# Attention steps in twos, the projection ahead of the weighted sums, and routing in short operations

## The chip, the cores and the metric

The kernel runs on one core of a Trainium2 chip. Its time is that of one execution on the device, in microseconds (us). PE is the matrix engine (TensorE), DVE the vector engine, ACT the scalar engine, POOL the GpSimd engine, and SP the engine that issues most of the DMAs. Each engine works through its own queue in the order in which the program was written.

## What is computed

Attention over 4 batches of 8 heads, 768 tokens, head size 64, in which a query sees only the keys whose six sign bits (of a projection on six columns) agree with its own; then a mixture of experts on the result:

```python
q_bits = (einsum('bhsd,dk->bhsk', q, proj) > 0)
k_bits = (einsum('bhsd,dk->bhsk', k, proj) > 0)
mask = q_bucket[:, :, :, None] == k_bucket[:, :, None, :]
scores = where(mask, q @ k.T / sqrt(64), -1e9)
attn = softmax(scores)
x = (attn @ v) as (3072, 512)
e_idx = argmax(x @ w_gate)
for each expert e:
    out[rows of e] = gate * sigmoid(x @ w_output_gate)[e] * (relu(x @ w1[e]) @ w2[e])
```

All in 32-bit floats; the scores are matched to that with two-part operands (a high and a low half).

## The kernel before

**The attention stage** works on 16 pairs of heads. A pair has 12 steps of 128 queries by 768 keys, so there are 192 steps (`NSTEP`), in 32 blocks of six (`PER`). For one step s:

- `scores(s)` (L538) is the score tile, called S below: eight matmuls (four products, each as two that run side by side in the two 64-row halves of the array) fill the two banks of a `ps_s` tile. DVE's minimum (L550) brings it to SBUF as `sc` and gives each row's smallest value. There are two `ps_s` tiles, used in turn.
- `soft` (L553) is ACT's exponential in place, with the row sums; `normal` (L562) is for two steps: DVE adds up the sums and takes the reciprocal (L565, L566), and POOL scales both tiles (L568).
- `transposed(s - 6, ...)` (L570), called T below, turns the scaled tile of six steps earlier: twelve matmuls with the identity (L589), six to a 64-row half, each half into a bank of its own. The first half always goes to one of two `ps_t` banks, the second to `ps_m` or `ps_a` (or `ps_t`). Two ACT copies (L595), of the second half first, bring them to `pts`.
- `weighted` (L598), called W below, makes the weighted sums of the block before, once per block: six column blocks for each of the two heads j=0 and j=1, side by side, in a `ps_a` bank; DVE copies the result to `ot` (L609).

The order of all this is written out by hand in one loop over the steps (L972 to L1002): S of the step, then, at the first step of a block (k == 0), five exponentials, the scalings and W, then T of six steps earlier, then whatever was planned for this step. Two lists carry everything else: `plan(step, fn)` runs a function after the step's T; `block(step, when, fn)` runs it at a block's first step, at the place named by `when`. Before the change these places are "early" and "amid" (ahead of and between the scalings), then "logits", "matmuls" (W, and behind it the projection) and "behind" (DMAs).

What else the steps carry, and what the change touches:

- `project` (L432): the sign bits of a later pair of heads, four matmuls into `ps_m`, a threshold on DVE (L443), then the bits' DMAs in `spread` (L525).
- `routing(b)` (L628): for each batch but the last its experts' logits (L640), their transposes in `tokens` (L650), the best expert (`best`, `choose`), the prefix sums over tokens (`prefix`, L707 to L712), ranks, positions (`table_chunks`, `table_pos`) and the table that lists each expert's tokens (`table_rhs`, `table_hot`, `table_sum` L238, `table_add` L241). They are planned at fixed steps counted from the batch's end, s0.
- From step 168 on (`late`), the first expert is chosen (`compare`, `pick`, `chosen`), its first weights are loaded and split in eight pieces on POOL (`early_w1`, L917 and L918), and its first tokens are gathered and turned (`early_gather`, `early_turn`).
- `rows` (L611) puts finished sums into `xb` (DVE, two buffers) and from there into `x_dram` by SP's DMAs.

The experts proper, which follow the attention stage, are not touched.

## Time and profile before

| | us |
|---|---|
| median of 3 runs (lowest to highest) | 725.77 (725.47 to 726.86) |
| the profiled execution, its own time | 729.64 |
| its span, first to last instruction | 727.8 |
| PE busy | 713.2 (98%) |
| DVE, ACT, POOL busy | 462.6, 456.1, 398.5 |

The span is one execution as the hardware profiler saw it, 1.8 us shorter than that execution's own time. A row of the timeline gives an instruction's start, its duration, its engine and line, what it writes and reads, and in brackets how long the engine stood idle before it and what ended that. Matmuls overlap, and the ends of PE's instructions are modelled, so the distance between two starts says more than a duration.

### The profile page before, as it was taken

Reading aid. Unit: us, or ns where it says so; the run is one execution under the profiler, and the core shown is the slowest. Engines: PE = TensorE matmul, PEld = TensorE weight load, DVE = VectorE, ACT = ScalarE, POOL = GpSimd, SP = SyncE. Lnnn points to the kernel's source line nnn. Section 1 sums busy time; section 2 is a strip of 40 time slices with the busy share of each in tenths; the row PEclk is TensorE's granted clock in tenths of the full one; section 3 lists DMA queues with packets and bytes.
Section 4 is the critical chain, followed back from the end, with each engine's and each line's share of the span. In section 5 each row is a group of like instructions: output and inputs, shape, how many; then the busy total and the mean of one; then the engine's idle time right before and its main releaser. Section 6 shows DMA issues by size and latency. Waiting matters only on the chain. (4 is left out here: it accounts for less than half of the span.)

```text
span 727.8 us, 17398 instructions
## 1 busy us (share of the span) xinstructions
PE 713.2 (98%) x6591; PEld 584.1 (80%) x6591; DVE 462.6 (64%) x1008; ACT 456.1 (63%) x927; POOL 398.5 (55%) x489
## 2 busy tenths in 40 slices
PE   8999999999999999999999999999999999999996
PEld 5777785777777777767686689789999999989894
DVE  7877776887767886868976672373554546455440
ACT  5898988898889897988888212442434343434331
POOL 5767756566565666564689525517173636465201
PEclk9999999999999999999999899999999999999998
DMA  5554553444354444542534322744445353537401
GB/s 171 149 129 104 123 129 91 110 104 107 102 126 88 99 121 94 120 102 68 128 61 113 117 68 79 269 137 155 145 135 172 114 189 129 187 118 236 160 11 42
DMA packets 85284, 89.20 MB, mean 123 GB/s; under 512 B 57167, under 2 KB 67591, under 8 KB 85192
## 3 DMA queue, kind: packets, MB, share of 16 engines
q1 hardware_dynamic: 79704, 74.59, 38.3%
q0 software_dynamic: 5200, 13.31, 5.5%
q8 instruction: 54, 0.88, 0.5%
q14 instruction: 38, 0.31, 0.2%
q10 hardware_dynamic: 288, 0.10, 0.1%
HBM read 59.57 MB, written 13.11 MB: 100 GB/s over the span
## 5 line engine op out<-in xcount | busy, mean ns | idle before, releaser
L568 POOL TENSOR_SCALAR sc<-sc,rsum 128x768 f32<-128x768 f32 x192 | 173.2, 916 | 137.3 <-PE ps_a L589 76.8
L550 DVE TENSOR_SCALAR_CACHE_REDUCE sc<-ps_s 128x768 f32<-128x768 f32 x192 | 183.4, 956 | 48.4 <-PE ps_s L547 43.7
L558 ACT ACTIVATE sc<-sc,mn 128x768 f32<-128x768 f32 x192 | 178.4, 937 | 5.3 <-DVE sc L550 5.3
L547 PE MATMUL ps_s<-kh,qhl 64*128 64x384 f32 x768 | 152.2, 379 | 0.6 <-DVE sc L550 0.6
L606 PE MATMUL ps_a<-pts,vt 128*64 128x384 f32 x768 | 137.4, 490 | 0.0
L589 PEld LDWEIGHTS ps_t<-ident,sc 64*128 64x128 f32 x1236 | 95.9, 140 | 26.8 <-POOL sc L568 16.4
L606 PEld LDWEIGHTS ps_a<-pts,vt 128*64 128x64 f32 x768 | 68.6, 137 | 57.6 <-issue 13.9
L595 ACT COPY pts<-ps_t 128x384 f32<-128x384 f32 x203 | 98.0, 490 | 14.8 <-PE ps_t L589 14.8
L589 PE MATMUL ps_t<-ident,sc 64*128 64x64 f32 x1236 | 104.6, 226 | 2.3 <-POOL sc L568 1.6
L335 DVE SCALAR_TENSOR_TENSOR hl<-ps_s,hh 128x256 fp32r<-128x256 f32 (+8 forms) x40 | 34.0, 849 | 107.9 <-ACT hh L334 82.5
L324 PE MATMUL ps_s<-xh,w1h 128*128 128x256 f32 (+7 forms) x288 | 97.3, 338 | 0.0
L345 POOL DMA_INDIRECT out_dram<-yo,sid x29 | 31.1, 1074 | 119.8 <-ACT yo L342 81.1
L324 PE MATMUL ps_s<-xlo,w1h 128*128 128x256 f32 (+7 forms) x288 | 95.7, 332 | 0.0
L324 PE MATMUL ps_s<-xh,w1l 128*128 128x256 f32 (+7 forms) x288 | 95.4, 331 | 0.0
L298 POOL DMA_INDIRECT xq<-x_dram,idx x75 | 81.7, 1089 | 23.8 <-issue 21.3
L334 ACT ACTIVATE hh<-ps_s 128x256 fp32r<-128x256 f32 (+8 forms) x40 | 29.1, 726 | 99.0 <-PE ps_s L324 71.8
L547 PEld LDWEIGHTS ps_s<-kh,qhl 64*128 64x128 f32 x768 | 81.1, 190 | 4.8 <-DVE sc L550 1.7
L547 PE MATMUL ps_s<-bb 64*128 64x384 f32 x384 | 69.3, 338 | 0.0
L547 PE MATMUL ps_s<-kl,qhl 64*128 64x384 f32 x384 | 68.4, 335 | 0.0
L595 ACT COPY pts<-ps_a 128x384 f32<-128x384 f32 x109 | 52.3, 480 | 24.9 <-PE ps_a L589 21.4
L589 PE MATMUL ps_a<-ident,sc 64*128 64x64 f32 x654 | 59.3, 224 | 1.9 <-DVE ot L609 1.9
L589 PEld LDWEIGHTS ps_a<-ident,sc 64*128 64x128 f32 x654 | 54.2, 138 | 4.4 <-DVE ot L609 2.9
(224 smaller groups left out, 1368.5 us busy)
## 6 DMA issues: line engine op xcount, KB each, us to landing
w_raw<-in_w_dram SPq DMA_DIRECT2D x34, 512.0 KB
qk<-in_qkT_dram SPq DMA_DIRECT2D x32, 384.0 KB
qhl<-qhl SPq DMA_DIRECT2D x62, 192.0 KB
xh<-in_w_dram SPq DMA_DIRECT2D x14, 512.0 KB
xlo<-in_w_dram SPq DMA_DIRECT2D x14, 512.0 KB
vt<-in_v_dram SPq DMA_DIRECT2D x16, 384.0 KB
x_dram<-xb SPq DMA_DIRECT2D x60, 96.0 KB
bb<-bt SPq DMA_DIRECT2D x62, 36.0 KB
```

What stands on the lines that cost most here:

```text
L298: nc.gpsimd.indirect_dma_start(out=xq[:, k * P:(k + 1) * P], out_offset=None, in_=x_dram.rearrange("n (a f) -> (n a) f", a=NB32), in_offse ...
L324: nc.tensor.matmul(ps, l, r, start=first and k == 0, stop=last and k == len(pairs) - 1)
L334: nc.scalar.activation(hh, ph, AF.Relu)
L335: return lambda: nc.vector.scalar_tensor_tensor(hl, ph, 0.0, f32(hh), ALU.max, ALU.subtract)
L345: nc.gpsimd.indirect_dma_start(out=out[:, :], out_offset=bass.IndirectOffsetOnAxis(ap=sid[0:n, r, a:a + 1], axis=0), in_=yo[0:n], in_offse ...
L547: nc.tensor.matmul(ss[:, h, 0:HS], q[rs, c:c + P], k[rs, 0:HS], start=(i == 0), stop=(i == 3))
L550: nc.vector.tensor_scalar(sc, ss[:, :, 0:HS], MASKED, None, ALU.min, ALU.min, accum_out=mn)
L558: nc.scalar.activation(pr, pr, AF.Exp, bias=mn, scale=-1.0, accum_out=sums[s // GROUP][:, k, 0:1])
L568: nc.gpsimd.tensor_scalar(live[s0 + k], live[s0 + k], rs[:, k:k + 1], 0.0, ALU.mult, ALU.add)
L589: nc.tensor.transpose(trs[h][:, c], pr[r, c * P:(c + 1) * P], ident[r, r])
L595: (nc.vector.tensor_copy if h and last else nc.scalar.copy)(pts[:, :, t * P + h * hq:t * P + (h + 1) * hq], trs[h])
L606: nc.tensor.matmul(st["av"][j * D:(j + 1) * D], st["v"][:, j, c], blocks[hb][j][:, c], start=(c == 0), stop=(c == NT - 1))
```

## The change

- The loop runs over pairs of steps from step 6 on: S, S, then (at a block's first pair) the exponentials, the projection, the routing's matmuls and W, then T, T, then both steps' plans. All six exponentials of a block come at its first pair.
- The second half of the first T of a block goes to a `ps_s` tile, and DVE, not ACT, copies it; the others take `ps_m` in steps 1, 2 and 4 of a block and `ps_a` in 3 and 5. `sc` gets an eighth buffer; `xb` loses one of two, and the positions' table `t_ob` shares the logits' tile `lt`.
- The projection is at place "before" (ahead of W, behind S), in a `ps_t` bank. So are the logits, the tokens' transposes, the prefix sums and the table's sum, tokens and table in `ps_t` banks.
- The routing's DVE and POOL work is cut into shorter functions, planned by a list of steps (`ROUTE`).
- The choice of the first expert, its loads and its eight pieces on POOL get other steps.

```diff
+        ROUTE = ((18, "best"), (18, "equal"), (20, "lowest"), (20, "one_hot"), (24, "own_ranks"), (26, "chunk_hot"),
+                 (28, "chunk_pos"), (30, "gate_sums"), (32, "hot0"), (33, "column2"), (34, "gate_values"),
+                 (38, "hot1"), (38, "column0"), (39, "column1"), (40, "hot2"))
...
-            sc = tp.tile([P, 2, HS], F32, name="sc", bufs=LAG + 1)
+            sc = tp.tile([P, 2, HS], F32, name="sc", bufs=LAG + 2)
...
-                second = (ps_t, "ps_t") if last or s in held and s % PER == 0 else (
-                    ps_m, "ps_m") if s % 2 == 0 and s not in held else (ps_a, "ps_a")
-                trs = [pool.tile([P, HS], F32, name=name) for pool, name in ((ps_t, "ps_t"), second)]
+                trs = [ps_t.tile([P, HS], F32, name="ps_t")]
+                if s % PER == 0 and not last:
+                    trs.append(ps_s.tile([P, 2, 512], F32, name="ps_s")[:, 0, 0:HS])
+                else:
+                    pool, name = (ps_t, "ps_t") if last else (ps_m, "ps_m") if s % PER in (1, 2, 4) else (ps_a, "ps_a")
+                    trs.append(pool.tile([P, HS], F32, name=name))
...
-                (nc.vector.tensor_copy if h and last else nc.scalar.copy)(
+                (nc.vector.tensor_copy if h and (last or s % PER == 0) else nc.scalar.copy)(
...
-                st["xb"] = gp.tile([P, S // 32, 32], F32, name="xb", bufs=2)
+                st["xb"] = gp.tile([P, S // 32, 32], F32, name="xb", bufs=1)
...
+            def hot_part(h):
+                st["ob"] = table_hot(gp, st["pos"], NT, st.get("ob"), h * NT // 3, (h + 1) * NT // 3)
...
-                    block(s0 - PER, "matmuls", lambda g=g: project(g))
-                    held.add(s0 - PER - LAG)
+                    block(s0 - PER, "before", lambda g=g: project(g, ps_t.tile([P, HS], F32, name="ps_t")))
...
-                block(s0 + PER * (hf + 1), "logits", lambda r=r, hf=hf: r["logits"](hf, H // 2))
-            block(s0 + 3 * PER, "amid", r["choose"])
-            if b < B - 2:
-                block(s0 + 4 * PER, "amid", r["gate_sums"])
-                block(s0 + 5 * PER, "amid", r["gate_values"], r["chunk_pos"])
-            else:
-                block(s0 + 5 * PER, "amid", r["gate_sums"], r["gate_values"], r["chunk_pos"])
-            plan(s0 + 34, r["columns"])
-            block(s0 + 6 * PER, "amid", r["hot"])
-            for n, fn in ((s0 + 8, lambda r=r: r["tokens"](0, H // 2)), (s0 + 14, lambda r=r: r["tokens"](1, H // 2)),
-                          (s0 + 15, r["best"]), (s0 + 20, r["prefix"]), (s0 + 21, r["offsets"]),
-                          (s0 + 22, r["own_ranks"]), (s0 + 23, r["chunk_hot"]),
-                          (s0 + 38, r["table"]), (s0 + 39, r["entries"])):
-                plan(n, fn)
+                block(s0 + PER * (hf + 1), "before", lambda r=r, hf=hf: r["logits"](hf, H // 2))
+            for n, when, name in ((12, "before", "tokens0"), (18, "before", "tokens1"), (24, "before", "prefix"),
+                                  (24, "before", "offsets"),
+                                  (42, "before", "table"), (42, "before", "entries")):
+                block(s0 + n, when, r[name])
+            for n, name in ROUTE:
+                plan(s0 + n, r[name])
...
-        block(late, "amid", compare, pick, chosen)
-        plan(late + 16, early_gather)
+        plan(late + 1, compare)
+        plan(late + 2, pick, chosen)
+        plan(late + 18, early_gather)
...
-            plan(late + (0, 1, 15, 18)[cc], lambda cc=cc: early_load(cc))
+            plan(late + (2, 3, 11, 15)[cc], lambda cc=cc: early_load(cc))
             for h in range(2):
-                plan(late + 12 + (1, 2, 3, 5)[(2 * cc + h) % 4] + PER * (cc // 2), lambda cc=cc, h=h: early_w1(cc, h))
+                plan(late + (8, 10, 13, 14, 16, 19, 20, 22)[2 * cc + h], lambda cc=cc, h=h: early_w1(cc, h))
...
+            for s in range(PER, NSTEP + LAG, 2):
+                k = s % PER
+                both = range(s, s + 2)
+                for x in both:
+                    if x < NSTEP:
+                        live[x] = scores(x)
+                        raw.append(x)
+                if k == 0 and s > PER:
                     softs(2)
                     now("early")
                     normals()
                     now("amid")
                     softs(2)
                     normals()
-                    for when in ("logits", "matmuls", "behind"):
+                    for when in ("before", "matmuls", "behind"):
                         now(when)
-                    softs(0 if s in few else 1)
-                elif k == 4:
+                    softs(1)
+                elif k == 4 or s == PER:
                     normals()
-                if s >= LAG:
-                    transposed(s - LAG, live.pop(s - LAG))
-                if k == 2 and s > 2 * PER or s - 1 in few or PER < s < 2 * PER and k in (1, 2, 4):
+                for x in both:
+                    transposed(x - LAG, live.pop(x - LAG))
+                if s < 2 * PER or k == 0:
                     softs(1)
-                for fn in at.get(s, ()):
-                    fn()
+                for x in both:
+                    for fn in at.get(x, ()):
+                        fn()
```

## Rows read from the trace of the kernel before

**Rows 1.** Windows: stretch, its length, then busy us of PE, PEld, DVE, ACT, POOL, clock, DMA.
```profile
20.00:395.00 375.00, 371.58 (x4666) 277.66 (x4662) 289.05 (x753) 326.12 (x751) 241.18 (x324) 1.00 0.46 108
395.00:410.20 15.20, 13.63 (x124) 10.39 (x123) 7.39 (x16) 9.30 (x18) 14.90 (x15) 0.78 0.59 165
```
**Rows 2.** PE timeline of a steady step: start us, duration us, engine, line, operation.
```profile
251.72 0.21 PE L589 MATMUL ps_t<-ident,sc 64*128 64x64 f32 x1
...
251.78 0.22 PE L589 MATMUL ps_t<-ident,sc 64*128 64x64 f32 x1
...
252.06 0.42 PE L547 MATMUL ps_s<-kh,qhl 64*128 64x384 f32 x2
...
252.85 0.21 PE L589 MATMUL ps_t<-ident,sc 64*128 64x64 f32 x1
```
**Rows 3.** PE timeline: the weighted sums of a block behind logits, and without them.
```profile
221.94 4.09 PE L606 MATMUL ps_a<-pts,vt 128*64 128x384 f32 x24
...
246.25 4.36 PE L606 MATMUL ps_a<-pts,vt 128*64 128x384 f32 x24
```
**Rows 4.** PE timeline at start-up: the last of two score tiles in a row.
```profile
17.52 0.34 PE L547 MATMUL ps_s<-kh,qhl 64*128 64x384 f32 x2
...
18.22 0.53 PE L589 MATMUL ps_t<-ident,sc 64*128 64x64 f32 x12
```
**Rows 5.** ACT timeline ahead of the sums at 246.25.
```profile
245.61 0.48 ACT L595 COPY pts<-ps_a 128x384 f32<-128x384 f32 x1 [0.30 <-PE ps_a L589]
245.99 0.48 ACT L595 COPY pts<-ps_t 128x384 f32<-128x384 f32 x1
```
**Rows 6.** Waits from 100 to 395: who, for whom: us in total, times, longest.
```profile
DVE sc L550 <- PE ps_s L547: 35.2, 77, 1.9
...
PEld ps_a L606 <- ACT pts L595: 8.4, 23, 0.6
...
PE ps_a L589 <- DVE ot L609: 1.9, 4, 1.1
```
**Rows 7.** PE timeline: a transposition followed by the tokens' transposes.
```profile
228.27 0.28 PE L589 MATMUL ps_t<-ident,sc 64*128 64x64 f32 x2
...
228.76 0.55 PE L650 MATMUL ps_m<-ident,lt 128*128 128x128 f32 x3
```
**Rows 8.** DVE timeline: score minima.
```profile
18.30 0.95 DVE L550 TENSOR_SCALAR_CACHE_REDUCE sc<-ps_s 128x768 f32<-128x768 f32 x1
...
253.05 0.96 DVE L550 TENSOR_SCALAR_CACHE_REDUCE sc<-ps_s 128x768 f32<-128x768 f32 x1
...
366.49 0.96 DVE L550 TENSOR_SCALAR_CACHE_REDUCE sc<-ps_s 128x768 f32<-128x768 f32 x1 [0.60 <-PE ps_a L589]
367.37 0.08 DVE L550 DVE_READ_ACCUMULATOR sc<-ps_s 128x1 f32 x1
367.37 0.95 DVE L550 TENSOR_SCALAR_CACHE_REDUCE sc<-ps_s 128x768 f32<-128x768 f32 x1
```
**Rows 9.** DVE timeline: the routing's longer operations.
```profile
138.15 0.56 DVE L680 TENSOR_TENSOR oneh<-ei,expi 128x48 f32<-128x48 f32 x1
138.75 0.84 DVE L683 CAST ohb<-oneh 128x48 bf16<-128x48 f32 x1
...
345.33 0.81 DVE L202 TENSOR_TENSOR t_ge<-rank,chki 128x30 f32<-128x30 f32 x1
346.18 0.44 DVE L205 TENSOR_TENSOR t_oa<-t_ge 128x24 f32<-128x24 f32 x1
```
**Rows 10.** PE timeline behind the last scores.
```profile
402.74 0.90 PE L589 MATMUL ps_t<-ident,sc 64*128 64x64 f32 x12 [1.57 <-POOL sc L568]
```
**Rows 11.** POOL timeline behind the last scores.
```profile
399.81 0.63 POOL L917 TENSOR_SCALAR w1h<-w_raw 128x512 fp32r<-128x512 f32 x1
...
401.77 3.55 POOL L568 TENSOR_SCALAR sc<-sc,rsum 128x768 f32<-128x768 f32 x4
```
**Rows 12.** PE timeline at start-up: a score tile that waited for its bank.
```profile
19.30 0.44 PE L547 MATMUL ps_s<-kh,qhl 64*128 64x384 f32 x2 [0.56 <-DVE sc L550]
```

More of the change, by code (lines that the diff above doesn't have):

```diff
@@ L646, in tokens @@
                     st["lgt"] = gp.tile([P, NT, 2 * E], F32, name="lgt")
-                pm = ps_m.tile([P, 3, H // 2, 32], F32, name="ps_m")
+                pm = ps_t.tile([P, 3, H // 2, 32], F32, name="ps_t")
                 for t in range(3):
@@ L672, in best, with equal, lowest, one_hot @@
                 nc.scalar.activation(st["en"], lgt[:, :, E:2 * E], AF.Exp, scale=-1.0)
-            def choose():
-                eq = gp.tile(bc, F32, name="eq")
+            def equal():
+                st["eq"] = eq = gp.tile(bc, F32, name="eq")
                 nc.vector.tensor_scalar(eq, st["df"], 0.0, None, ALU.is_equal)
                 nc.vector.tensor_tensor(eq, eq, expi[:, None, :].broadcast_to(bc), ALU.mult)
-                ei = gp.tile([P, NT], F32, name="ei")
-                nc.vector.tensor_reduce(ei, eq, AX.X, ALU.min)
-                nc.vector.tensor_tensor(oh, ei[:, :, None].broadcast_to(bc),
+            def lowest():
+                st["ei"] = ei = gp.tile([P, NT], F32, name="ei")
+                nc.vector.tensor_reduce(ei, st["eq"], AX.X, ALU.min)
+            def one_hot():
+                nc.vector.tensor_tensor(oh, st["ei"][:, :, None].broadcast_to(bc),
                                         expi[:, None, :].broadcast_to(bc), ALU.is_equal)
@@ L683, in choose @@
                 nc.vector.tensor_copy(st["ohb"], oh)
+            def choose():
+                equal()
+                lowest()
+                one_hot()
             def gate_sums():
@@ L739, in places, with columns, column @@
                 chunk_pos()
-            def columns():
-                st["rhs"] = table_rhs(gp, st["oa"], oh, gate[:, ts], toki[:, ts], NT, nc.vector if b == B - 1 else nc.gpsimd)
+            def columns(which=(2, 0, 1)):
+                st["rhs"] = table_rhs(gp, st["oa"], oh, gate[:, ts], toki[:, ts], NT,
+                                      nc.vector if b == B - 1 else nc.gpsimd, st.get("rhs"), which)
+            def column(i):
+                columns((i,))
             def cols():
@@ L756, in entries @@
                 table_add(tacc_e, st["pt"])
-            fns = dict(logits=logits, tokens=tokens, add_pair=add_pair, best=best, choose=choose,
+            fns = dict(equal=equal, column0=lambda: column(0), column1=lambda: column(1), column2=lambda: column(2),
+                       tokens0=lambda: tokens(0, H // 2), tokens1=lambda: tokens(1, H // 2), lowest=lowest, one_hot=one_hot, hot0=lambda: hot_part(0), hot1=lambda: hot_part(1),
+                       hot2=lambda: hot_part(2), logits=logits, tokens=tokens, add_pair=add_pair, best=best, choose=choose,
                        gates=gates, prefix=prefix, ranks=ranks, cols=cols, hot=hot, table=table, entries=entries,
@@ L787, in lsh_attention_then_moe @@
                 plan(4, lambda: project(1))
-                held.add(0)
                 plan(5, lambda: split_lo(1, 0, 0), lambda: spread(1, 0))
@@ L824, in lsh_attention_then_moe @@
         for hf in range(2):
-            block(s0 + PER * (hf + 1), "logits", lambda hf=hf: r["logits"](hf, lp))
-            plan(s0 + PER * (hf + 1) + 2, lambda hf=hf: r["tokens"](hf, lp))
-            held.add(s0 + PER * (hf + 1) + 2 - LAG)
+            block(s0 + PER * (hf + 1), "before", lambda hf=hf: r["logits"](hf, lp))
+        block(s0 + 2 * PER, "before", lambda: r["tokens"](0, lp))
+        plan(s0 + 2 * PER + 5, lambda: r["tokens"](1, lp))
         late = 12 * (H // 2) * (B - 1) + 24
@@ L951, in lsh_attention_then_moe @@
             raw = []
-            few = []
             def softs(n):
@@ L970, in now @@
                     fn()
-            for s in range(NSTEP + LAG):
-                k = s % PER
-                if s < NSTEP:
-                    live[s] = scores(s)
-                    raw.append(s)
+            for s in range(PER):
+                live[s] = scores(s)
+                raw.append(s)
                 if 0 < s < 3:
                     turn_idle(3)
-                if s < PER:
-                    normals()
-                    softs(1)
-                elif s < 2 * PER:
-                    if k in (0, 4):
-                        normals()
-                elif k == 0:
+                normals()
+                softs(1)
+                for fn in at.get(s, ()):
+                    fn()
[7 more added lines that the diff above has]
+                if k == 0 and s > PER:
                     softs(2)
```

27 lines of the change are left out of this document (15 added, 12 removed).

## The prediction

> **What bounds the kernel now.** I read the windows first, then the PE timeline of one steady step, then what PE waits for, then the queues that feed it. Between 20 and 395 us the attention stage keeps PE at work for 371.6 of 375.0 us at the full clock [rows 1]; DVE (289 us) and ACT (326 us) have room. So PE's own order is the bound, and 3.4 us at most are plain idle. A PE that counts as busy may still be badly ordered, so I went into the step. A scaled tile's transposition (T, twelve matmuls) takes 0.34 us from its first start (251.72) to the first score matmul; the score tile (S, eight matmuls) takes 0.79 us from there (252.06) to the next T (252.85): 1.13 us a step [rows 2]. The other part of a six-step block is the weighted sums (W, 24 records), 4.36 us; where the logits' matmuls stand in front of W it lasts 4.09 us [rows 3].
>
> **The change, part by part.** The sum is made in the profiled execution's time, 729.64 us, which is 0.5% above the median of 725.77.
>
> *Twos.* Where S follows S with no T between (start-up), it takes 18.22 - 17.52 = 0.70 us, not 0.79 [rows 4]: going over from T to S costs 0.09. Two transposition pairs within T start 0.06 apart [rows 2], so a T followed by T takes 6 x 0.06 = 0.36, not 0.34. Two steps therefore go from 2 x 1.13 = 2.26 to 0.36 + 0.34 + 0.79 + 0.70 = 2.19 us. There are three such pairs in a block and 31 blocks with both kinds of work: 93 x 0.07 = **6.5 us gained**. Bounds: 0.09 each if the second T also takes 0.34 (8.4 gained), and 0.02 each lost if S behind S stays at 0.79 in the steady stretch (1.9 lost). I take 6.5, since both pitches have rows.
>
> *W starts clean.* W's first half (j=0) and second half (j=1) run side by side; j=1 needs the last ACT copy of the block's last T. That copy starts at 245.99 and lasts 0.48, so it ends at 246.47, 0.22 us after W's first matmul at 246.25 [rows 3, 5]: the halves start staggered, and W ends late by that. The trace has 23 such waits of PE on ACT's copies [rows 6], and the W behind logits, whose copies are long done, is 0.27 us shorter. After the change two S stand between the last T and W. Copies run at a pitch of 0.38 [rows 5], and a T's first copy starts 0.26 us after the T: at 245.61, where the S in front of W had begun some 0.9 us before 246.25. The first T of a pair ends 0.36 before the first S, so four copies start 0.10 before that S and end 3 x 0.38 + 0.48 later, at 1.52; the two S last 0.79 + 0.70 = 1.49 us, and the step over to W comes on top. The stagger goes: 23 x 0.27 = **6.2 us gained**; bounds 0 (the copies come later) and 6.2.
>
> *Small matmuls ahead of W.* T followed by the routing's transposes takes 0.49 us (228.27 to 228.76) [rows 7] against 0.34 in front of S [rows 2]. Fourteen such places (seven of tokens, three of prefix, three of the table sum, one of logits) move to between S and W, where the step from S to other work is paid already: 14 x 0.15 = **2.1 us gained**; bounds 0 and 2.1. The projection's matmuls, threshold on DVE and bits stay as many; only their place moves by one W. Its bits and the DMAs behind them ("behind", on SP) come no later than before.
>
> *Routing in short operations.* In the new order a pair lasts 2.19 us and holds two score minima on DVE at a pitch of 0.88 (366.49 to 367.37) [rows 8], so 2.19 - 1.76 = 0.43 us are free per pair; anything longer planned in a pair whose scores come next delays PE. The steps with number 18 and 24 of a batch fall behind W, where DVE has time; those of 28, 34 and 40 fall ahead of W, which covers them. Exposed are one_hot at 20 (0.56 + 0.84, at POOL's side, less 0.43: 1.0) and chunk_hot at 26 (0.81 + 0.44 - 0.43 = 0.8), three times each [rows 9]: 5.4 us. The choice of the expert is exposed once before and once after, and cancels. What these replace is the idle time of now, 3.4 us [rows 1]: **2.0 us lost**. Bounds: 3.4 gained (nothing exposed) and 5.4 lost (nothing of today's idle time goes).
>
> *POOL at the end of attention.* After the last scores PE waits 1.57 us for POOL's scaled tiles (402.74) [rows 10]; POOL had a piece of the first expert's weights (its first operation at 399.81) in front of the last four scalings, which start 1.96 us later at 401.77 [rows 11]. The mean granted clock from 395 to 410.2 is 0.78 [rows 1]: some 6.7 of these 15.2 us went at 1.2 GHz instead of 2.4, which can have cost at most half of that, 3.3 us. The change puts two of the eight pieces a block earlier and leaves three, not four, in the last one; its loads move with them on SP's queue (steps 2, 3, 11, 15 of that stretch), behind the choice's register load, with nothing else urgent behind. I count the piece's 1.96 us and a third of the slow clock, 1.0 us: **3.0 us gained**; bounds 0 and 5.3.
>
> *At nothing.* One of twelve ACT copies per block goes to DVE. DVE does it behind W's own copy, while two T run; if DVE is late there, see the third rival. ACT's six exponentials now stand together around W; ACT works for 326.1 of 375 us today [rows 1] and gives 31 copies of 0.48 away, so 311 us of work meet a stretch of some 362 us, and it still fits. The one buffer of xb waits for DMAs issued a block (11 us) earlier; the shared tile "lt" is written again 14 steps after its last reader.
>
> Sum: -6.5 - 6.2 - 2.1 + 2.0 - 3.0 = -15.8, so 713.8 us profiled; scaled to the median, 725.77 x 713.8 / 729.64 = **710.0 us**.
>
> **Where a page would say otherwise.** The pair is tight on DVE. S's first tile is done 0.79 us after its start, DVE begins 0.20 later (252.85 to 253.05), and the bank is free 1.00 after DVE's start (18.30 to 19.30) [rows 2, 8, 12]. The second minimum thus starts at 0.99 + 0.88 = 1.87 and frees its bank at 2.87; the next pair wants it at 2.19 + 0.79 = 2.98. Slack: 0.11 us. The Trainium skill, page "VectorE: DVE Perf Modes", section "The DRAIN you can't avoid", says that the next DVE operation does not start until the pipe of the one before is empty. By that, the pitch would be no less than the operation's 0.95 us with its accumulator read of 0.08, the bank would be free at 0.99 + 1.03 + 1.00 = 3.02, and two pairs of each block would stall by 0.04: 62 x 0.04 = 2.5 us lost. The trace disagrees: 0.88 is less than the operation's own 0.95 to 0.96, so the sum goes by 0.88.
>
> **The rivals.** *DVE paces the pairs.* If a minimum costs 1.03 and each pair also carries a small operation's 0.3 us (the reciprocal of the sums, a routing step), DVE needs 2 x 1.03 + 0.3 = 2.36 against 2.19: 0.17 lost in the two pairs per block that no W covers, 62 x 0.17 = 10.5, so 724.3 profiled, 720.5. For it: the slack is 0.11 and bursts leave no second reserve. Against: in the steady stretch DVE sat waiting for PE's scores 77 times, 35.2 us [rows 6]. Chance 0.15.
>
> *It doesn't do what it says.* S behind S stays at 0.79 and W keeps its stagger, because the copies of two T crowd against it: without 6.5 and 6.2 the change is -3.1, so 726.5 profiled, 722.7. Against: both have rows. Chance 0.06.
>
> *The borrowed score bank, slower than before.* The block's first T now writes half into a score bank, DVE must empty it, and the block's fourth S needs that bank. DVE's copy stands behind the sums' copy, and both behind whatever DVE waits for (POOL's split, ACT's exponentials). Counted from W's end, S wants the bank at 0.70 + 0.79 = 1.49 us (two T, one S), and a DVE on time frees it at about 0.20 + 2 x 0.48 = 1.16 us (an estimate: DVE's start behind PE from [rows 8], its copies taken like ACT's of the same size [rows 5]). What DVE is late beyond 0.33 stops PE in each of 31 blocks; 0.33 + 15.8/31 = 0.84 is the point from which the kernel gets slower. The trace has PE waiting for the sums' copy up to 1.1 us, four times in all [rows 6]. If that became the rule: 31 x (1.1 - 0.33) = 23.9 lost, 737.7 profiled, 733.8. Against: four times in some 25 blocks, not each. Chance 0.08.
>
> **How the numbers follow.** The forecast, 710.0 us, has 0.71. The unknown terms move it by -3 to +8 us by themselves. The range, 704 to 724 us, takes these in, with the first rival and the second; the third is left out. A difference under 0.2% (1.5 us) is about what a measurement of this kernel can't tell from none. Faster 0.86 (forecast, first rival, most of the second), same 0.05, slower 0.09.
>
> **What would show it.** Right: S behind S at 0.70 and pairs of 2.19 us in the PE timeline; W at 4.1 us in nearly all blocks; no PE waits on ACT's copies ahead of W; attention's last scores some 12 us earlier than now; a higher clock in the last block. DVE's sums' copy starting with W's end in each block speaks against the third rival. Wrong: PE waiting for DVE at the second S of a pair (first rival), W still at 4.36 (second), or PE waiting at the fourth S of each block for a DVE copy of transposed scores (third).

## The result and the profile after

The changed kernel takes **718.44 us** (median of four runs, 716.74 to 719.31) against 726.32 us of the kernel before on the same chip: a ratio of 0.989 [0.9866, 0.9914]. The time lies inside the range and has the sign that was forecast, but the gain of 7.9 us is half of the 15.8 us of the sum. The profiled execution took 719.2 us, with a span of 717.5.

The windows of the changed kernel (stretch, its length, busy us of PE, PEld, DVE, ACT, POOL, clock, DMA) answer to [rows 1], with two more at the start:
```profile
20.00:395.00 375.00, 369.10 (x4725) 261.25 (x4725) 302.20 (x797) 314.74 (x729) 248.37 (x332) 1.00 0.47 111
395.00:410.20 15.20, 14.41 (x137) 10.82 (x136) 11.63 (x23) 5.11 (x12) 6.95 (x7) 1.00 0.40 119
16.00:20.00 4.00, 2.74 (x29) 2.13 (x25) 3.75 (x9) 2.67 (x6) 2.35 (x3) 1.00 0.61 208
20.00:24.00 4.00, 3.60 (x39) 3.55 (x41) 2.81 (x9) 2.27 (x5) 2.34 (x4) 0.62 0.56 117
```
PE is still the bound. ACT fell from 326 to 315 us (311 by the sum) and DVE rose from 289 to 302. The slow clock behind 395 us is gone (1.00 for 0.78; the same work comes some 6 us earlier now, and from 385 to 425 us the clock is 1.00 throughout), but a new stretch at 0.62 has come up between 20 and 24 us.

The PE timeline of the changed kernel (start us, duration us, engine, line, operation, idle time before it and what ended it):
```profile
15.25 0.85 PE L444 MATMUL ps_m<-qk,pjc 128*32 128x384 f32 x8
...
18.63 0.44 PE L552 MATMUL ps_s<-kh,qhl 64*128 64x384 f32 x2 [0.91 <-DVE sc L555]
20.40 0.27 PE L597 MATMUL ps_s<-ident,sc 64*128 64x64 f32 x1 [0.75 <-DVE sc L555]
...
30.10 1.19 PE L614 MATMUL ps_a<-pts,vt 128*64 128x384 f32 x6
...
64.35 4.09 PE L614 MATMUL ps_a<-pts,vt 128*64 128x384 f32 x24
...
71.35 0.43 PE L552 MATMUL ps_s<-kh,qhl 64*128 64x384 f32 x2
...
72.13 0.35 PE L552 MATMUL ps_s<-kh,qhl 64*128 64x384 f32 x2
...
72.85 0.21 PE L597 MATMUL ps_m<-ident,sc 64*128 64x64 f32 x1
...
73.57 0.42 PE L552 MATMUL ps_s<-kh,qhl 64*128 64x384 f32 x2
...
74.35 0.44 PE L552 MATMUL ps_s<-kh,qhl 64*128 64x384 f32 x2
...
75.24 0.54 PE L614 MATMUL ps_a<-pts,vt 128*64 128x384 f32 x2
...
142.47 0.45 PE L552 MATMUL ps_s<-kh,qhl 64*128 64x384 f32 x2 [0.69 <-DVE sc L555]
...
395.86 0.58 PE L597 MATMUL ps_s<-ident,sc 64*128 64x64 f32 x12 [0.21 <-POOL sc L573]
```
Four things are to be read here. In the steady pair (71.35 to 73.57) S lasts 0.78, the S behind it 0.72 and the two T 0.72: 2.22 us, where two single steps take 2.26 by [rows 2]. The pair ahead of the sums lasts longer: 0.78 and 0.89 (73.57 to 75.24). The sums last 4.09 us, as the clean ones of [rows 3]; from their start to that of the next T it is 4.02, and 4.29 where they are staggered, and block lengths below are counted from start to start of the sums. And three of these rows wait for DVE: two at the start, one behind the transpositions of step 18 (142.47); the wait of 1.57 us of [rows 10] is now 0.21.

The waits from 100 to 395 us (who, for whom: us in total, times, longest), which answer to [rows 6]:
```profile
DVE sc L555 <- PE ps_s L552: 14.3, 27, 1.3
...
PE ps_s L552 <- DVE sc L555: 4.1, 9, 0.7
...
PEld ps_a L614 <- ACT pts L603: 1.0, 4, 0.3
```
The sums' wait for ACT's copies went from 8.4 to 1.0 us. DVE's reserve, read as its waiting for scores, went from 35.2 to 14.3 us, and PE now waits for DVE (4.1 us) where it did not before.

Step 18 on DVE, and what POOL did meanwhile, first DVE's timeline and then POOL's:
```profile
139.74 0.20 DVE L674 TENSOR_REDUCE mx<-lgt 128x6 f32<-128x48 f32 x1
139.97 1.11 DVE L676 TENSOR_TENSOR df<-lgt,mx 128x48 f32<-128x48 f32 x1
...
141.33 0.21 DVE L685 TENSOR_TENSOR eq<-eq,expi 128x48 f32<-128x48 f32 x1
```
```profile
140.00 1.02 POOL L511 TENSOR_TENSOR kl<-qk,kh 128x384 fp32r<-128x384 f32 x1
```
A difference of 48 elements per partition takes 1.11 us and ends (141.08) just behind POOL's subtraction (141.02); its neighbour of the same size (L685) takes 0.21. The next score minimum on DVE starts only at 141.46, behind both, and PE's next bank comes free with it (142.47 in the PE timeline).

### The profile page after: what moved, and what is told of

The parts are those of the page before. It is cut to its first block, busy times and chain, and to the rows that moved or that the text cites. A ratio compares the mean times of both kernels' runs of the same rounds, so it can differ in the third digit from the quotient of the medians.

```text
span 717.5 us, 17378 instructions
## 1 busy us (share of the span) xinstructions
PE 700.2 (98%) x6591; PEld 560.0 (78%) x6591; DVE 473.5 (66%) x1045; ACT 439.2 (61%) x896; POOL 397.2 (55%) x489
## 3 DMA queue, kind: packets, MB, share of 16 engines
q1 hardware_dynamic: 79704, 74.59, 38.5%
## 5 line engine op out<-in xcount | busy, mean ns | idle before, releaser
L555 DVE TENSOR_SCALAR_CACHE_REDUCE sc<-ps_s 128x768 f32<-128x768 f32 x192 | 176.3, 954 | 24.6 <-PE ps_s L552 21.3
L552 PE MATMUL ps_s<-kh,qhl 64*128 64x384 f32 x768 | 144.7, 370 | 5.6 <-DVE sc L555 5.6
L614 PE MATMUL ps_a<-pts,vt 128*64 128x384 f32 x768 | 131.1, 490 | 0.0
L614 PEld LDWEIGHTS ps_a<-pts,vt 128*64 128x64 f32 x768 | 52.2, 137 | 66.6 <-issue 59.2
L597 PEld LDWEIGHTS ps_t<-ident,sc 64*128 64x128 f32 x1152 | 83.6, 140 | 20.8 <-POOL sc L573 11.4
L597 PE MATMUL ps_t<-ident,sc 64*128 64x64 f32 x1152 | 88.6, 224 | 0.7 <-POOL w1h L933 0.7
L552 PEld LDWEIGHTS ps_s<-kh,qhl 64*128 64x128 f32 x768 | 75.1, 189 | 17.1 <-DVE sc L555 12.4
L603 ACT COPY pts<-ps_m 128x384 f32<-128x384 f32 x93 | 44.7, 481 | 26.1 <-PE ps_m L597 20.4
L327 PEld LDWEIGHTS ps_s<-xh,w1h 128*128 128x128 f32 x288 | 54.1, 188 | 2.0 <-issue 0.6
L327 PEld LDWEIGHTS ps_s<-xlo,w1h 128*128 128x128 f32 x288 | 54.1, 188 | 1.3 <-DVE xlo L284 0.2
```

The costliest lines, as they stand in the source:

```text
L327: nc.tensor.matmul(ps, l, r, start=first and k == 0, stop=last and k == len(pairs) - 1)
L552: nc.tensor.matmul(ss[:, h, 0:HS], q[rs, c:c + P], k[rs, 0:HS], start=(i == 0), stop=(i == 3))
L555: nc.vector.tensor_scalar(sc, ss[:, :, 0:HS], MASKED, None, ALU.min, ALU.min, accum_out=mn)
L597: nc.tensor.transpose(trs[h][:, c], pr[r, c * P:(c + 1) * P], ident[r, r])
L603: (nc.vector.tensor_copy if h and (last or s % PER == 0) else nc.scalar.copy)(pts[:, :, t * P + h * hq:t * P + (h + 1) * hq], trs[h])
L614: nc.tensor.matmul(st["av"][j * D:(j + 1) * D], st["v"][:, j, c], blocks[hb][j][:, c], start=(c == 0), stop=(c == NT - 1))
```

## The experiments

Labels stand for kernels; all times are medians, and each ratio is to the kernel before on the same chip.

### e1: the first transposition without a score bank

```diff
-                if s % PER == 0 and not last:
+                if s and s % PER == 0 and not last:
```


> The changed kernel, but the very first transposition puts its second half into the bank that the sums use later, not into a score bank. Theory (at the start a score bank is held for the transposition, the tensor engine waits 0.91 and 0.75 us for DVE's minima, and its clock falls to 0.62 behind that): the first weighted sums start at some 28.3 us of the span instead of 30.1, the clock in 20 to 24 us is near 1.00, and the kernel is about 1.8 us faster than the changed one: 716.6 us, 0.9865 of before. Rival (the two scores together ask too much of DVE there, whatever the bank): the waits stay, the first sums start within 0.3 us of 30.1, the time is the changed kernel's, 0.989.

Measured: **715.01 us, 0.9862 [0.9841, 0.9883]**. PE timeline of e1:
```profile
15.75 0.85 PE L444 MATMUL ps_m<-qk,pjc 128*32 128x384 f32 x8
...
19.12 0.45 PE L552 MATMUL ps_s<-kh,qhl 64*128 64x384 f32 x2 [0.91 <-DVE sc L555]
...
19.93 0.21 PE L597 MATMUL ps_a<-ident,sc 64*128 64x64 f32 x1
...
28.55 0.87 PE L614 MATMUL ps_a<-pts,vt 128*64 128x384 f32 x4
```
The second wait (0.75 us) is gone, the first stays, the clock from 20 to 24 us is 1.00, and the first sums start at 28.55. The numbers are the theory's, but they can't be taken at face value: the first projection, ahead of all this, starts anywhere between 13.8 and 16.2 us in the profiles of this case. Counted from there to the first sums it is 14.85 us in the changed kernel and 12.80 here.

### e2: score, transposition, score, transposition in two pairs of three

```diff
+                turns = k != 0 and 2 * PER < s < NSTEP
+                if turns and k == 4:
+                    normals()
                 for x in both:
                     if x < NSTEP:
                         live[x] = scores(x)
                         raw.append(x)
+                    if turns:
+                        transposed(x - LAG, live.pop(x - LAG))
...
-                for x in both:
+                for x in () if turns else both:
                     transposed(x - LAG, live.pop(x - LAG))
```


> The changed kernel, but in the second and third pair of each block the order is score, transposition, score, transposition again; only the pair around the weighted sums keeps its twos. Theory (each going over from a transposition to scores costs 0.07 to 0.09 us of the tensor engine): 30 blocks x 2 pairs x 0.07 = 4.2 us slower than the changed kernel, a block without projection at 11.03 us instead of 10.89, and the sums stay at 4.02 us: 722.6 us, 0.995 of before. Rival (all of the steady gain came from the sums' clean start): within 1 us of the changed kernel, 0.989.

Measured: **723.92 us, 0.9987 [0.9973, 1.0002]**, 7 us slower than the changed kernel by the ratios, more than the theory allowed. PE timeline, then DVE timeline of e2, ahead of one block's sums (the first S of their pair starts at 73.57):
```profile
74.59 0.45 PE L552 MATMUL ps_s<-kh,qhl 64*128 64x384 f32 x2
...
75.50 0.54 PE L614 MATMUL ps_a<-pts,vt 128*64 128x384 f32 x2
```
```profile
74.46 0.08 DVE L555 DVE_READ_ACCUMULATOR sc<-ps_s 128x1 f32 x1
```
A block is 0.32 us longer (two blocks 23.20 for 22.57). Of that 0.26 lies in the two S ahead of the sums: they last 1.93 us (73.57 to 75.50) for 1.67, and the second starts at 74.59, 0.05 after DVE has read out (74.46 to 74.54) the minimum of the bank that it fills. With only one T ahead of them, these two S catch up with DVE. What is left is 0.06 for two pairs, 0.03 for going over once more in each, less than half of the theory's price.

### e3: the kernel before, the projection ahead of the sums

```diff
-                    block(s0 - PER, "matmuls", lambda g=g: project(g))
+                    block(s0 - PER, "logits", lambda g=g: project(g))
```


> The kernel before, with one line changed: the projection's matmuls stand in front of the weighted sums, not behind them. Theory (the sums start staggered because their second half waits for the copies of the transposition just ahead; anything in between hides it): the sums of the 15 blocks with a projection fall from 4.36 to about 4.05 us, 15 x 0.3 = 4.5 us less: 721.8 us, 0.994 of before. Rival (the place of the projection is indifferent, the sums are shortened only by two scores ahead of them): 1.000 of before, the sums at 4.3.

Measured: **743.27 us, 1.0248 [1.0224, 1.0271]**: the mechanism was right, the sign wrong. PE timeline of e3:
```profile
63.05 4.09 PE L606 MATMUL ps_a<-pts,vt 128*64 128x384 f32 x24
...
74.08 4.36 PE L606 MATMUL ps_a<-pts,vt 128*64 128x384 f32 x24
...
113.54 1.50 PE L640 MATMUL ps_m<-ot,wgt 128*32 128x384 f32 x8 [4.37 <-DVE bt L443]
```
The sums behind a projection (63.05) last 4.09 us and the others (74.08) 4.36: a projection between the last T and the sums makes them clean, which the single S that stands there in both does not. But projection and logits share the one buffer ps_m: where both come ahead of the same sums, the logits wait 4.37 us until DVE has read the projection, three times, 13.1 us in all. With each of these waits the granted clock falls too (0.64 from 112 to 116 us, 0.70 from 220 to 224, 0.50 from 322 to 326), so the waits are not the whole loss. That is why the change needs the projection in the transposing bank; the sum had called this a mere change of place.

### e4: the kernel before, profiled again

No edit. 

> The kernel before, unchanged, profiled once more, for its last 35 us. The first profile had 0.78 of the clock between 395 and 410 us and the whole run was 3.3 us above its own median. Theory A (the loss of the clock belongs to the kernel): the clock is again below 0.85 there and from the last weighted sums to the end it takes within 1 us of 332.6. Theory B (it fell only in that execution): near 1.00, and some 3 us less behind the last sums, so that 1 to 3 us of what the two profiles show as gained in the tail are no gain of the change.

Measured: **724.62 us** in the one run, span 722.8. Its window, and from its PE timeline the first projection, the first sums, and two sums whose distance (11.17 us) is a block without a projection:
```profile
395.00:410.20 15.20, 13.64 (x134) 9.65 (x132) 9.05 (x14) 7.92 (x16) 14.43 (x13) 0.89 0.58 164
```
```profile
14.31 0.85 PE L439 MATMUL ps_m<-qk,pjc 128*32 128x384 f32 x8
...
26.30 1.18 PE L606 MATMUL ps_a<-pts,vt 128*64 128x384 f32 x5
...
72.78 4.35 PE L606 MATMUL ps_a<-pts,vt 128*64 128x384 f32 x24
...
83.95 4.36 PE L606 MATMUL ps_a<-pts,vt 128*64 128x384 f32 x24
```
The clock behind 395 us is 0.89 this time, and from the thirty-first sums to the end it takes 329.4 us (722.8 - 393.4), not 332.6; e3 has 329.2. So the profile on which the forecast rests was some 3 us slow in its tail, which is theory B in part: both profiles of the kernel lose clock there, and how much differs between executions. More than half of the 3 us lies behind the last sums, where the change does nothing (317.7 us to the end for 315.9 here). From the first projection to the first sums, on the other hand, the kernel before takes 12.0 us in both of its profiles, and so does e3.

### e5: the routing's DVE work under the sums

Beside e1's edit:
```diff
-        ROUTE = ((18, "best"), (18, "equal"), (20, "lowest"), (20, "one_hot"), (24, "own_ranks"), (26, "chunk_hot"),
+        ROUTE = ((18, "exps"), (20, "lowest"), (20, "one_hot"), (24, "own_ranks"), (26, "chunk_hot"),
...
-                 (38, "hot1"), (38, "column0"), (39, "column1"), (40, "hot2"))
+                 (36, "hot1"), (38, "column0"), (39, "column1"), (40, "hot2"))
...
-            for n, when, name in ((12, "before", "tokens0"), (18, "before", "tokens1"), (24, "before", "prefix"),
+            for n, when, name in ((12, "before", "tokens0"), (18, "before", "tokens1"), (18, "before", "best_df"), (18, "before", "equal"), (24, "before", "prefix"),
```
(best_df is the maximum and the difference of best, exps its two exponentials.) 

> The first run's kernel (transposition 0 in the sums' bank) with two pieces of the routing moved: the differences to the largest logit and the marks of equality (three DVE operations and the maximum) stand in front of the weighted sums of their block instead of behind the first transpositions, and the second third of the table's comparison moves from step 38 to 36. Theory (the stalls of 1.60 us behind the transpositions of step 18 and of 1.24 us at step 38 come from DVE operations in front of the scores' minima; under the sums they are free): 3 x (0.88 + 0.2) + 2 x 0.63 = 4.5 us faster than the first run's kernel, 710.5 us, 0.980 of before. Rival (under the sums they make DVE's copy of the sums late, and the fourth scores wait for the borrowed bank instead): within 1 us of the first run's kernel, 0.986, with waits of the tensor engine at the second score of the second pair.

Measured: **715.83 us, 0.9883 [0.9836, 0.9931]**: no gain over e1. DVE, POOL and PE timelines of e5:
```profile
137.41 0.70 DVE L691 TENSOR_SCALAR eq<-df 128x48 f32<-128x48 f32 x1
138.15 0.86 DVE L692 TENSOR_TENSOR eq<-eq,expi 128x48 f32<-128x48 f32 x1
```
```profile
135.36 3.59 POOL L573 TENSOR_SCALAR sc<-sc,rsum 128x768 f32<-128x768 f32 x4 [0.87 <-DVE rsum L571]
```
```profile
139.99 0.45 PE L552 MATMUL ps_s<-kh,qhl 64*128 64x384 f32 x2 [0.75 <-DVE pts L603]
```
The table's third was moved well: at 36 it takes 0.42 us for 1.25, and the two blocks of step 38 fall from 13.79 to 13.19 us. Step 18 went by the rival. POOL's four scalings stand under the sums; two DVE operations that take 0.2 us elsewhere take 0.70 and 0.86, each until about the end of a scaling, DVE's copy of the sums waits behind them, and the fourth S waits for the borrowed bank. This is the mechanism of the third rival.

### e6: POOL's subtraction two steps later

```diff
-                    plan(n + 3, lambda g=g, j=j: split_lo(g, j, 1, nc.gpsimd))
+                    plan(n + 5, lambda g=g, j=j: split_lo(g, j, 1, nc.gpsimd))
```


> The changed kernel with nothing of the routing moved: only POOL's subtraction of the low half of the keys (1.02 us) is issued two steps later in each block, at 5 instead of 3, so that it no longer runs beside the small DVE operations of steps 18 and 38. Theory (a DVE operation with two operands is held while POOL subtracts: 1.11 us beside it, 0.2 without): the difference takes 0.2 us, the gap between transpositions and scores at step 18 falls from 1.60 to about 0.8, the comparison at 38 from 1.25 to 0.42: 3 x 0.9 + 2 x 0.6 = 3.9 us faster than the changed kernel, 714.5 us, 0.9836. Rival (those operations are long by themselves, by their broadcast operands): they stay at 1.1 and 1.25, and the time within 1 us of the changed kernel's, 0.989.

Measured: **786.52 us, 1.0847 [1.0816, 1.0879]**. The experiment failed by its own making. Waits of e6, then POOL's timeline:
```profile
PE ps_s L552 <- POOL kl L511: 41.2, 14, 4.7
```
```profile
39.28 1.79 POOL L573 TENSOR_SCALAR sc<-sc,rsum 128x768 f32<-128x768 f32 x2 [4.28 <-ACT pts L603]
41.04 1.00 POOL L511 TENSOR_TENSOR kl<-qk,kh 128x384 fp32r<-128x384 f32 x1
```
At 3 the subtraction stands ahead of the block's last two scalings in POOL's queue, at 5 behind them; they wait 4.28 us, and the scores that read kl wait for POOL. It says how little can be moved on POOL. Its question, who holds the small DVE operations, went to e8.

### e7: POOL's pieces back

```diff
-            plan(late + (2, 3, 11, 15)[cc], lambda cc=cc: early_load(cc))
+            plan(late + (2, 3, 15, 18)[cc], lambda cc=cc: early_load(cc))
-                plan(late + (8, 10, 13, 14, 16, 19, 20, 22)[2 * cc + h], lambda cc=cc, h=h: early_w1(cc, h))
+                plan(late + (13, 14, 15, 17, 19, 20, 21, 23)[2 * cc + h], lambda cc=cc, h=h: early_w1(cc, h))
-        plan(late + 18, early_gather)
+        plan(late + 16, early_gather)
```
The gather at 16 comes ahead of the table's last entries, so it fetches rows by an unfinished table, with the same instructions. 

> The changed kernel with POOL's pieces of the first expert's weights and their loads at the steps of the kernel before (loads 3 and 4 at 15 and 18, pieces at 13 to 23, the gather at 16). Theory (the move is worth the wait for the last scaled tiles, and part of the clock that fell behind it): the wait of 1.57 us of the tensor engine ahead of the last transpositions comes back, and from the last full weighted sums to the end it takes 2 to 3 us longer than the changed kernel's 328.1: 720.9 us, 0.9925. Rival (the tail's gain has another cause, the clean order of the last block): within 0.5 us of the changed kernel, 0.989.

Measured: **719.03 us, 0.9925 [0.9899, 0.995]**, the theory's ratio. PE timeline of e7, then its window:
```profile
394.44 0.90 PE L597 MATMUL ps_t<-ident,sc 64*128 64x64 f32 x12 [1.56 <-POOL sc L573]
```
```profile
395.00:410.20 15.20, 15.20 (x126) 11.68 (x123) 10.55 (x19) 4.05 (x8) 6.23 (x7) 0.81 0.35 111
```
The wait of 1.57 us is back, and with it the fall of the clock (0.81). From the thirty-first sums to the end it takes 330.9 us (717.3 - 386.4), for 328.1 in the first profile of the changed kernel and 327.4 in the second (e10). The POOL term of the sum, with its cause, holds.

### e8: the routing's DVE work where POOL is idle

Beside e1's edit:
```diff
-        ROUTE = ((18, "best"), (18, "equal"), (20, "lowest"), (20, "one_hot"), (24, "own_ranks"), (26, "chunk_hot"),
+        ROUTE = ((18, "largest"), (20, "below"), (20, "equal"), (22, "lowest"), (22, "one_hot"), (24, "own_ranks"), (26, "chunk_hot"),
...
-                 (38, "hot1"), (38, "column0"), (39, "column1"), (40, "hot2"))
+                 (36, "hot1"), (38, "column0"), (39, "column1"), (40, "hot2"))
...
-        plan(late + 1, compare)
-        plan(late + 2, pick, chosen)
+        plan(late + 2, compare)
+        plan(late + 4, pick, chosen)
-            plan(late + (2, 3, 11, 15)[cc], lambda cc=cc: early_load(cc))
+            plan(late + (4, 5, 11, 15)[cc], lambda cc=cc: early_load(cc))
```
(largest is the maximum of best, below the rest of it.) 

> The first run's kernel (transposition 0 in the sums' bank) with the routing's DVE work spread to where POOL is idle: only the maximum stays at step 18, the differences and marks of equality go to 20, the lowest expert and its one-hot form to 22, the table's second third to 36; the expert's comparison goes to 2, its choice and the first loads to 4 and 5 of the last stretch. Theory (a small DVE operation with operands in SBUF is held until the POOL operation beside it ends; alone it takes 0.2 us): the difference takes 0.21 us instead of 1.11; the first run's stalls of 1.08 at step 18 and 0.63 at step 38 fall to 0.2 to 0.4 and to 0: 3 x 0.7 + 2 x 0.63 + some 0.6 for the choice = 4 us faster than the first run's kernel, 711 us, 0.981 of before. Rival (0.8 us of DVE work cost the tensor engine the same wherever they stand in a pair): only the 1.2 us of step 38 are gained, 713.8 us, 0.985.

Measured: **711.24 us, 0.9812 [0.9787, 0.9836]**, as the theory had it, and the best of this case together with e11. DVE's timeline, then POOL's:
```profile
139.12 0.20 DVE L682 TENSOR_TENSOR df<-lgt,mx 128x48 f32<-128x48 f32 x1
...
139.58 0.21 DVE L691 TENSOR_TENSOR eq<-eq,expi 128x48 f32<-128x48 f32 x1
...
142.19 0.78 DVE L701 CAST ohb<-oneh 128x48 bf16<-128x48 f32 x1
```
```profile
136.97 1.01 POOL L511 TENSOR_TENSOR kl<-qk,kh 128x384 fp32r<-128x384 f32 x1
142.01 1.80 POOL L573 TENSOR_SCALAR sc<-sc,rsum 128x768 f32<-128x768 f32 x2 [4.03 <-DVE ei L695]
```
With POOL idle (137.98 to 142.01) the difference takes 0.20 us for 1.11. The one operation that fell beside a scaling, the cast at 142.19, takes 0.78 and ends at 142.97, just behind the first of the two scalings (142.91). The block of step 18 lasts 11.73 us for 12.28, that of step 38 13.18 for 13.79, and the one where the expert is compared 10.97 for 12.22.

### e9: the twos undone

```diff
+                turns = 2 * PER < s < NSTEP
+                def step(x):
+                    live[x] = scores(x)
+                    raw.append(x)
-                for x in both:
+                for x in (both if not turns else (s,) if k == 0 else ()):
                     if x < NSTEP:
-                        live[x] = scores(x)
-                        raw.append(x)
+                        step(x)
...
                 for x in both:
+                    if turns and (k or x > s):
+                        step(x)
                     transposed(x - LAG, live.pop(x - LAG))
```


> The changed kernel with the twos alone undone: from the third block on one score tile, then one transposition, as in the kernel before, the weighted sums behind the first score tile of a block; banks, routing and projection stay as changed. As forecast (0.07 us per pair, and a staggered start of the sums where no projection or routing stands in front): 30 x 3 x 0.07 + 14 x 0.27 = 10 us slower than the changed kernel, 728.5 us, 1.003 of before. By the rows of the two traces (transpositions and scores of a block last 6.88 us before and 6.85 after, so the twos themselves are worth 0.03 us per block): 30 x 0.03 + 14 x 0.27 = 4.7 us slower, 723.1 us, 0.9955; where DVE work is in the way it may even get faster, since a single score tile asks less of DVE at once.

Measured: **718.65 us, 0.9922 [0.989, 0.9953]**, beside 0.9882 of the changed kernel (e10). PE timeline of e9:
```profile
72.29 4.35 PE L614 MATMUL ps_a<-pts,vt 128*64 128x384 f32 x24
...
84.30 4.09 PE L614 MATMUL ps_a<-pts,vt 128*64 128x384 f32 x24
```
The sums behind a projection (84.30) stay clean, those behind a single S (72.29) have their stagger back. Blocks last 10.95 and 12.01 us for 10.90 and 11.67; without sums and projection 6.93 (10.95 - 4.02) and 6.93 (12.01 - 4.29 - 0.79), for 6.88 and 6.86: the twos by themselves are worth 0.05 to 0.07 us per block, not 0.21. In all it costs 3 us by the ratios, less than both readings. The routing's block of step 18 is faster without twos (11.94 for 12.28), as the last words of the expectation had it; and only seven sums are staggered, not 14, five of 4.35 us and two of 4.22. The others are clean with a single S ahead of them.

### e10: the changed kernel again

No edit. 

> The changed kernel once more, beside the two runs above. If its time belongs to the kernel: 0.987 to 0.991 of before, W's first start at 29 to 30 us with the clock at about 0.6 between 20 and 24 us, 359.3 us from the first full sums to the thirty-first, and 327 to 328 us from there to the end. If the start is a matter of the single execution: W's first start near 28 with the full clock.

Measured: **717.01 us, 0.9882 [0.9857, 0.9907]**. PE timeline:
```profile
13.78 0.85 PE L444 MATMUL ps_m<-qk,pjc 128*32 128x384 f32 x8
...
27.25 1.19 PE L614 MATMUL ps_a<-pts,vt 128*64 128x384 f32 x6
```
From the first projection to the first sums it takes 13.47 us, and the clock from 20 to 24 us is 1.00; 358.5 us to the thirty-first sums, 327.4 to the end. So the start costs 1.5 us more than before in every execution (13.47 to 13.50 here, in e7 and in e9), and where the clock falls as well 2.8 (14.85 in the first profile, 14.79 in e2; it fell in e6 too). With e1's edit it is 12.75 to 12.80 in e1, e5 and e8, and the clock from 20 to 24 us did not fall in any of them.

### e11: the first pair taken apart

Beside e8's edits:
```diff
-                for x in both:
+                for x in both[:1] if s == PER else both:
                     if x < NSTEP:
...
                 for x in both:
+                    if x == PER + 1:
+                        step(x)
                     transposed(x - LAG, live.pop(x - LAG))
```
(step(x) is the score tile of x, as in e9.) 

> The kernel of the spread-out routing with one more change: the first two scores that stand in front of transpositions (tiles 6 and 7) are taken apart again, tile 6, first transposition, tile 7, second transposition. From the first projection to the first weighted sums it took 12.0 us in the kernel before, 13.5 or 14.8 in the changed one, 12.8 with the first transposition's half in the sums' bank. Theory (what is left, 0.8 us, is the second of the paired scores waiting for DVE's minimum where no sums stand in between): 12.0 to 12.2 us, some 0.7 us less in all: 710.5 us, 0.980 of before. Rival (the rest comes from the later pairs or the routing's new banks): 12.6 to 12.9 us, and the time stays at 711.2.

Measured: **711.4 us, 0.981 [0.9792, 0.9829]**; from projection to sums 13.49 us, longer than e8's 12.75. PE timeline:
```profile
17.55 0.44 PE L552 MATMUL ps_s<-kh,qhl 64*128 64x384 f32 x2 [0.51 <-DVE sc L555]
...
19.33 0.44 PE L552 MATMUL ps_s<-kh,qhl 64*128 64x384 f32 x2 [0.43 <-DVE sc L555]
...
20.92 0.44 PE L552 MATMUL ps_s<-kh,qhl 64*128 64x384 f32 x2 [0.63 <-DVE sc L555]
```
A miss for both: the one wait of 0.9 us became three of 0.4 to 0.6. At the start DVE is the bound (busy for 3.97 of the 4 us from 16 on, here as in e8), and taking one pair apart only moves where PE meets it. What the last 0.8 us of the start hang on stays open.

## Why the prediction was half right

The steps are set against the second profile of before (e4, 722.8 us of span, at its median) and that of after (e10, 713.1; this execution took 714.77 us, 2.2 under its median).

- **Twos: forecast 6.5, measured about 2; this is the step that failed.** The 0.07 per pair was made of rows that are each right: S behind S takes 0.70 to 0.72, T behind T 0.72 in all. But the step before is 1.12 (0.78 and 0.34), so the pair gains 0.02 to 0.04; and the pair ahead of the sums gains nothing, since its second S takes 0.89, as the single S ahead of the sums did before (0.9). Transpositions and scores of a block without projection take 6.88 us before (11.17 - 4.29) and 6.88 after (10.90 - 4.02), with one 7.01 (12.08 - 4.29 - 0.78) and 6.86: 0.08 on average, 2.4 us in 31 blocks. e9 gives 0.05 to 0.07. A difference of two small numbers of 0.01 precision was multiplied by 93.
- **W starts clean: forecast 6.2, measured 6.4** (24 of 31 sums from 4.29 to 4.02). The price of a stagger was right; the count was luck. The 23 waits of [rows 6] are those of 100 to 395 us only, and seven of them stand ahead of sums that were clean already (221.94 of [rows 3] is one); 16 of them, and eight staggered sums outside of that stretch, make the 24. The cause is right in part: the two S were to hide the last copies, but in e9, with one S, only seven sums are staggered, so most of the 24 owe their clean start to the projection, as in e3, or the routing's matmuls ahead of them.
- **Small matmuls ahead, routing: forecast 0.1 gained, measured 0.2 to 0.3 a batch.** The eight blocks of a batch last 98.8 us before and 96.4 after; of the 2.4, 2.2 are sums and twos. So the net was about right, and the places wrong: step 20 exposes 0.1 to 0.2 us for the 1.0 of the sum and step 26 nothing for 0.8 (its block lasts 11.66 to 11.68, as one with a projection and no routing), while step 18, "behind W, where DVE has time", exposes about 1 us and step 38, which the sum doesn't name, 0.6. The sum took DVE's durations without asking what POOL does beside them.
- **The start: forecast nothing, measured 1.5 us lost, 2.8 where the clock falls.** The third rival had priced the borrowed bank behind the sums, where it came to nothing (no such wait in the changed kernel's steady stretch). Ahead of the first sums nothing covers DVE, and there it decides. By the count from the first projection e1 takes back 0.7 of it. Whether it also keeps the clock up is likely, not shown: it fell in none of four profiles with the edit and in three of six without. The whole times (0.9862 against 0.989 and 0.9882) are too close to tell.
- **POOL at the end: forecast 3.0, measured 1.3 to 2.0** (329.4 to 328.1 or 327.4). e7 shows the term itself at 2.8 to 3.5; but the loss of clock of [rows 1] was larger in that one execution than in the next. The tail can't be read closer than that: behind the last sums, where nothing was changed, it takes 315.9 us in e4 and 317.3 or 316.1 in the changed kernel. Between the last two sums, where POOL's pieces stand, 13.5 us became 10.8 or 11.3, and 15.0 in e7.
- **The range's frame.** The profiled execution was 3.9 us above the median, and scaling the sum by 0.995 doesn't take out what was lost in one place.

Together: 8.6 us gained between the first and the thirty-first sums (367.1 to 358.5) for 12.8 forecast, 2.0 in the tail, 1.5 lost at the start and 0.5 not the change's (the first projection came earlier in e10): 9.6, for 9.7 between the two spans. By e10's median and that of the kernel before beside it the gain is 7.6; the 2.2 us by which e10's execution is under its median lie between.

Of the rivals, the first (DVE paces the pairs) did not come as priced, 0.17 in two pairs. In the pair ahead of the sums DVE is close: its accumulator is read out at 74.20 to 74.29, and the second S that needs the bank starts at 74.35. In e2 PE runs into it there; that it costs the changed kernel anything in this place is not shown, since the profile has no wait there and an S ahead of the sums took 0.9 us before as well. The minima's pitch stayed at 0.88, as in [rows 8] (72.44 to 73.32). The bound that the prediction drew from the Trainium skill's page "VectorE: DVE Perf Modes", section "The DRAIN you can't avoid", did not come; the section itself adds that a next operation that isn't held starts earlier. The second rival fell in the half on the sums, which did lose their stagger; its other half is near in size, with twos worth about 2 of the 6.5, but not in cause: S behind S did take 0.70 to 0.72.

## What to carry to other kernels

Cost a reordering from the whole block on both sides, not from the best rows of each step: a gain of some hundredths per step has to be larger than the rounding of the rows it comes from. When small operations are moved on an engine, look at what the neighbour does in that very place; here the same operation costs 0.2 or 1.1 us, and spreading such operations to where the neighbour is idle was worth 3.8 us (e1 to e8, with the choice of the first expert spread out as well). And a borrowed buffer that is free behind a long stage has to be checked at the start, where that stage hasn't run yet.

## What the hardware showed

Small DVE operations on SBUF (differences, comparisons and casts of 48 elements per partition) that come while a POOL operation runs are held until about its end: 1.11 us beside a subtraction that ends at 141.02 (the changed kernel), 0.70 and 0.86 beside four scalings (e5), 0.78 beside a scaling (e8), 0.20 and 0.21 with POOL idle (e8). One that comes between two POOL operations is not held: e5's difference starts at 137.16, about where the second of the four scalings ends (135.36 and half of 3.59), and takes 0.21. Maxima, reciprocals and the minima, which read PSUM, keep their length beside POOL (the maximum L674 takes 0.20 at 139.74, while POOL scales until 140.0). The Trainium skill, page "SBUF — State Buffer", section "Who interferes with whom", says that DVE and GpSimd share one pair of ports, that an operation of DVE with two SBUF inputs, or in a two-port mode, contends for it with one of GpSimd that reads SBUF, and that whichever comes second stands still until the first is done. The durations above agree with it, the ports themselves no run shows; it would have put the routing's stalls in the right place.

Where PE waits at the start, the clock fell in some executions. In the three profiles in which it did (the changed kernel, e2 and e6), PE was busy for 2.74, 2.39 and 2.38 of the 4 us from 16 on, and the granted clock of the next 4 was 0.62, 0.62 and 0.66, between the levels of 1.2 and 2.4 GHz; in the changed kernel a score pair then took 2.72 us (21.28 to 24.00) for 1.50. In e10 PE was busy for 2.37 of these 4 us and the clock stayed at 1.00. What tells these executions apart, the runs don't show.
